# First group's second product wholly dense, and a new order, in a fused linear-attention and feed-forward kernel

## The chip, the cores and the metric

The kernel runs on one core of a Trainium2 chip. The metric is the device time of that core in microseconds, the median of the runs shown. Engines: TensorE (PE, with its weight loads PEld), VectorE (DVE), ScalarE (ACT), GpSimd (POOL) and SyncE (SP), on whose queue nearly all transfers are issued.

## What is computed

Linear attention with a cosine weighting, then two matrix products with a leaky relu between them. Eight batches, eight heads, 576 positions, 64 features per head; 4608 tokens of 512 go through 512 to 2048 to 512.

```python
def phi(x, c, s):
    r = np.maximum(x, 0.0)
    return np.concatenate([r * c, r * s], axis=-1)
q_p, k_p = phi(q, cos_w, sin_w), phi(k, cos_w, sin_w)
kv = np.einsum('bhsf,bhsd->bhfd', k_p, v)
z = np.sum(k_p, axis=2)
num = np.einsum('bhsf,bhfd->bhsd', q_p, kv)
den = np.einsum('bhsf,bhf->bhs', q_p, z)[..., None] + 1e-06
...
h = x @ w_in
g = np.maximum(0.01 * h, h)
return (g @ w_out).astype(np.float32)
```

## The kernel before

The tokens are worked in nine groups of 512: group g below 8 is the first 512 positions of batch g, group 8 the last 64 positions of all eight. Every operation has a short name, and a string `ORDER` lists all names in the order in which they are written into the program, with a letter for the engine where there is a choice (`:D` VectorE, `:A` ScalarE, `:P` GpSimd). Each engine, and the SP queue with its loads and stores, works its own part of that list strictly in order. Nothing else schedules.

The names, by stage:

- Loads: `Lq`, `Lk`, `Lv` bring a batch's q, k, v into one of four staging buffers in rotation (`stage`, 77 to 80 in the order listings), `Lw1.*` and `Lw2.*` the weights w_in and w_out. In groups 0 and 1 k and v come in halves a and b; in group 0 q too. A load into a buffer waits until the earlier content has been read.
- `q{g}.{j}.c` and `.s` (L246, L244) are relu times cosine or sine for token tile j of q, `k...` and `kp...` the same for k, `v...` the cast of v. `K` (L462, L474) sums k and v over the positions on TensorE, `kv` copies the sum out.
- `T{g}.{j}` transposes q on TensorE in groups 0 and 1 (L541), `tc` copies the transposed tile out; later groups do it by a transposing DMA, `Tq`. `N` multiplies q by kv (L562, L573), `D` divides by the denominator (three VectorE instructions, L582 to L586), `X` transposes the result (L598, L613), `xc` copies it out; from group 3 on a DMA, `Tx`, does that.
- First product of group 0: `M{m}` (L665), dense, 16 tiles of 128 rows of w_in; `a0` to `a7` (L674) are the leaky relus into the buffer G.
- First product of groups 1 to 8: `P{g}.{u}.{n}` (L763), seven products instead of eight, for four units u, each of four 256-column matmuls. Between them lie, per unit, the copies `b`, `s`, `u` and the sums `y`, `z` (L234, L238, L240), and the leaky relus `a`, `c`, `e`, `d` (L783). `b` copies the first product into another bank, `u` takes the sum after product 6, `z` and `y` add, and product 4 is added last, after `y`. `Xs`, `Ws` are the sums of inputs that the scheme needs.
- Second product of groups 1 to 8: `F{g}.{n}.{tt}.{h}` (L852), the same scheme over w_out, with sums `S` of G, `Tw` of w_out, copies and sums `t1`, `t2`, `t3`, results `r` and stores `st`.

Second product of group 0, before: w_out and G have 16 tiles to sum over. The first eight are done densely, `E{tt}.0` to `E{tt}.3`, each two matmuls of 512 columns (L688), for four token tiles tt in banks 4 to 7, and `ec{tt}` copies each bank to the result buffer `osb`. The other eight go by the seven products, `F0.n.tt.1`, four matmuls of 256 columns each, 14 operations, in banks 5 and 7; `S0.1h` to `S0.4h` are their sums of G, `t1.0`, `t2.0`, `t3.0` their chain, `r0.*` and `d0.*` add them to what lies in `osb`, and `st0.2` to `st0.5` store four quarters.

PSUM has eight banks of 512 columns: h0 (0, 1), h1 (2, 3), o (4, 5), n (6, 7), as the pools name them. `split.*` and `join.*` change whether two banks are one tile or two. In group 1 the units of the first product use banks by a list of their own, `FIRST_BANKS`, which takes all eight; from group 2 on they rotate through banks 0 to 3. `idle.at.n.id` (L378) are n matmuls of zeros into bank `at`, whose result nobody reads.

Of the kernel before, what the change touches and what calls it, by code (L numbers as in the profile page):

```python
# [20 lines left out]
setup blank:D Lq0b q0b.0.c:P Lk0b q0b.1.s:A Lq0a idle.5.14.0 k0b.1.c:A q0b.1.c:A kp0.3.s:D q0a.1.c:A Lk0a Lv0a  # L21
q0b.3.s:D q0a.1.s:A Lv0b k0b.7.c:D q0b.3.c:A q0a.3.s:D q0a.0.s:A q0b.2.c:P q0b.2.s:D q0a.3.c:A k0b.3.c:A
idle.4.11.1 T0.3 v0.1:A q0b.0.s:A q0a.0.c:D T0.1 k0b.0.c:P k0b.2.c:P T0.0 kp0.0.c:D q0a.2.c:P touch kp0.1.s:D
v0.0:A kp0.0.s:D kp0.1.c:D q0a.2.s:A tc0.1:D k0b.5.c:D k0b.8.c:A k0b.6.c:D tc0.0:D k0b.4.c:A kp0.2.s:D v0.3:P
Lw1.0 idle.5.2.2 K0a cw1.0:P kv0a:A v0.2:P T0.2 N0a.0 tc0.3:A tc0.2:D D0a.0 idle.5.6.3 K0b Lw1.2 Lw1.6 N0a.1
Lw1.1 Lw1.8 Lw1.3 kv0b:A N0b.0 X0a.0 D0a.1 idle.2.2.4 N0b.1 D0b.0 xc0a.0:A X0a.1 idle.2.2.5 X0b.0 M2.0.0
cw1.1:A M0.0.0 M1.0.0 M2.0.1 M0.0.1 xc0a.1:D M3.0.0 M3.0.1 xc0b.0:A D0b.1 cw1.3:D M2.1.0 Lw1.5 M2.1.1 cw1.6:P
Lw1.4 M1.0.1 cw1.2:A M3.1.0 cw1.5:P M0.1.0 M3.1.1 M0.1.1 M1.1.0 M2.0.2 X0b.1 xc0b.1:D M1.1.1 M2.0.3 M0.0.2
M0.0.3 Lq1 M1.0.2 M1.0.3 M0.1.2 cw1.4:D Lw1.7 M3.0.2 M0.1.3 M3.0.3 Ws0.1:D cw1.8:A Ws0.2:D M1.1.2 Ws0.4:D
M1.1.3 a0 M2.1.2 M4.0 Lw2.0 M2.1.3 q1.2.c:D M5.0 Lk1a M3.1.2 M3.1.3 a1 q1.0.s:D M6.0 M7.0 M6.1 M7.1 q1.1.s:D  # L30
M8.0 q1.0.c:D a3 cw1.7:D M8.1 M9.0 Lw2.1 M4.1 Lk1b M9.1 Ws0.3:D q1.3.s:A q1.3.c:A Ws1.1:D M10.0 M5.1 M10.1
M11.0 a4 q1.1.c:D M11.1 Ws1.2:D a2 M12.0 a5 cw2.0.0:D cw2.0.1:A M12.1 q1.2.s:A cw2.1.1:P M13.0 Lv1a M13.1
# [12 lines left out]
P1.2.3 y1.2:D F0.5.0.1 P1.3.2 u1.3:A v2.0:A s1.3:A c1.2 F0.5.1.1 v2.1:P t3.0:D k2.1.s:P d0.5:D k2.2.s:A P1.3.7
Tq2.1 Lk3 F0.4.0.1 S1.1l:D F0.4.1.1 P1.2.4 e1.2 d1.2 r0.5:D k2.0.c:D y1.3:D c1.3 F0.3.0.1 F0.3.1.1 d1.1 P1.3.3
r0.4:D join.n Lv3 r0.3:D P1.3.4 a1.3 z1.3:D S1.2l:D e1.3 S1.1h:D K2 d1.3 F1.1.0.0 kv2:A q3.2.s:A q3.1.s:A
q3.0.s:A F1.6.0.0 F1.1.0.1 S1.3l:D N2.0 F1.1.1.0 S1.2h:D q3.0.c:P F1.1.1.1 Lv3n D2.0 F1.6.0.1 t1.1:A q3.3.s:P
F1.6.1.0 st0.2 N2.1 S1.3h:D q3.3.c:A k3.2.s:P F1.6.1.1 D2.1 F1.2.0.0 t2.1:D F1.2.0.1 st0.3 k3.3.c:A q3.1.c:A
q3.2.c:A Lk3n v3.1:P N2.2 D2.2 Tw4.0:D F1.2.1.0 k3.0.s:A F1.7.0.0 Lq4 F1.2.1.1 F1.7.0.1 N2.3 k3.1.c:A D2.3  # L50
F1.7.1.0 r1.2:A F1.7.1.1 F1.5.0.0 X2.0 k3.2.c:A X2.1 t3.1:D X2.2 X2.3 v3.0:A S1.4l:D F1.5.0.1 xc2.0:D k3.1.s:A
k3.3.s:P F1.4.0.0 xc2.1:A F1.5.1.0 S1.4h:D P2.0.1 F1.4.0.1 Lk4 xc2.2:A k3.0.c:D xc2.3:D F1.5.1.1 b2.0:A
k3.4.c:A P2.0.2 Xs2.1:D Xs2.2:D P2.0.5 P2.0.6 Xs2.3:D k3.4.s:P K3 k4.0.s:P Tq3.0 a2.0 r1.5:D u2.0:A s2.0:D
P2.1.1 kv3:A Xs2.4:D z2.0:D P2.0.7 Tq3.1 k4.0.c:D P2.0.3 k4.1.s:D k4.4.c:A F1.3.0.0 N3.0 Lv4 k4.3.c:P k4.2.s:A
F1.3.0.1 y2.0:D P2.1.5 P2.0.4 e2.0 b2.1:A q4.1.c:A D3.0 P2.1.6 s2.1:A u2.1:A q4.0.s:P N3.1 q4.3.c:D D3.1 Lv4n
P2.1.2 P2.1.3 q4.1.s:P q4.3.s:D P2.1.7 F1.4.1.0 z2.1:D d2.0 F1.3.1.0 a2.1 c2.0 y2.1:D v4.0:P P2.2.5 N3.2
# [920 lines left out]
```

## Time and profile before

| what | value |
|---|---|
| median of 3 runs | 277.11 us (277.1 to 277.85) |
| profiled execution: its own time | 279.91 us |
| span in that profile | 278.1 us |
| TensorE busy | 266.3 us, 96% of the span |
| VectorE, ScalarE, GpSimd busy | 225.9, 192.9, 99.3 us |
| HBM read, written | 36.70 MB, 9.44 MB |
| TensorE's share of the chain that ended last | 76% |

Busy time of TensorE counts matmuls by modelled ends that overlap; a matmul of 256 columns lasts 0.27 us in the profile, but the next starts well before it ends. So the price of one in a row of equal ones is the spacing of the starts: the length of the row, less one duration, through the number less one.

Rows of a timeline give start, length, engine, line, operation, what it writes and reads, shapes and count; in brackets the idle time of that engine before it and what ended the wait. Rows of groups give the count, then busy us and mean ns of one.

### The profile page before, as it was taken

What the parts mean: (1) busy time and instruction counts of PE and PEld (TensorE: products, weight loads), DVE (VectorE), ACT (ScalarE), POOL (GpSimd) and SP (SyncE); (2) the same over time, 40 slices, a digit from 0 to 9 for tenths busy, and PEclk for the clock granted to TensorE, in tenths of its full rate; (3) what the DMA queues carried; (4) which work ended last, traced back from release to release, by engine and by line L of the source; (5) the groups of instructions that cost most, each with busy time, mean ns of one, the idle gap of its engine ahead of it and who ended that gap; (6) DMA issues with size and microseconds to landing.
All of it is one profiled execution on the core that took longest, in us unless ns stands there. A gap on an engine that the chain in (4) does not pass through costs nothing.

```text
span 278.1 us, 7012 instructions
## 1 busy us (share of the span) xinstructions
PE 266.3 (96%) x2813; PEld 232.6 (84%) x2813; DVE 225.9 (81%) x443; ACT 192.9 (69%) x342; POOL 99.3 (36%) x72
## 2 busy tenths in 40 slices
PE   6999999699999999999999999999999999999994
PEld 2566567498889999999999899989999999999983
DVE  1987989789999899989968998879878659866752
ACT  6757998599987887777868788647755555655400
POOL 4631062899375833963544265007100000000000
PEclk9999999799999999999999999999999999999999
DMA  6999999969899999999997996694455206101224
GB/s 231 382 390 383 374 304 347 290 201 247 265 286 170 323 212 230 335 170 261 294 333 127 245 175 217 131 213 116 82 106 154 79 2 151 57 21 40 77 61 131
DMA packets 88145, 57.08 MB, mean 205 GB/s; under 512 B 53808, under 2 KB 83504, under 8 KB 87600
## 3 DMA queue, kind: packets, MB, share of 16 engines
q1 hardware_dynamic: 87504, 56.11, 74.5%
q10 hardware_dynamic: 608, 0.52, 0.7%
q8 instruction: 22, 0.36, 0.5%
q14 instruction: 11, 0.09, 0.1%
HBM read 36.70 MB, written 9.44 MB: 166 GB/s over the span
## 4 chain that ended last, share of the span: by engine, by line
PE 76%; DMA 10%; DVE 7%; ACT 3%; issue 2%; SPq 1%; DVEq 0%; ACTq 0%
PE h L763 29%; PE o L852 29%; PE h L665 4%; DMA stage<-in_q_dram 3%; DMA stage<-in_v_dram 3%; PE n L562 2%; DMA qpT<-qp 2%; DMA xT<-xs 2%; PE n L474 2%; PE n L852 2%; DVE ext L234 1%; PE h L852 1%; ACT g L783 1%; DVE xs L586 1%; DVE h L234 1%
## 5 line engine op out<-in xcount | busy, mean ns | idle before, releaser
L783 ACT ACTIVATE g<-h 128x512 f16<-128x512 f32 x90 | 51.8, 598 | 28.9 <-PE h L763 14.3
L852 PEld LDWEIGHTS <-g 128*128 128x128 f16 x680 | 65.5, 98 | 7.3 <-issue 0.4
L852 PE MATMUL o<-w,g 128*128 128x256 f16 x504 | 68.6, 273 | 0.2 <-DVE osb L234 0.2
L763 PEld LDWEIGHTS <-w 128*128 128x128 f16 x512 | 55.8, 114 | 4.9 <-issue 3.4
L763 PE MATMUL h<-xT,w 128*128 128x256 f16 x356 | 51.0, 274 | 0.0
L763 PEld LDWEIGHTS <-wext 128*128 128x128 f16 x384 | 42.1, 114 | 1.4 <-issue 0.2
L852 PE MATMUL o<-T,ext 128*128 128x256 f16 x232 | 32.9, 273 | 0.4 <-DVE osb L234 0.4
L246 POOL TENSOR_SCALAR qp<-stage,sin_t 128x512 f16<-128x512 f32 x12 | 25.1, 2096 | 15.2 <-DVE xs L586 8.8
L246 POOL TENSOR_SCALAR qp<-stage,cos_t 128x512 f16<-128x512 f32 (+1 forms) x11 | 20.1, 1832 | 28.7 <-DMA stage<-in_q_dram 20.1
L852 PEld LDWEIGHTS <-ext 128*128 128x128 f16 x272 | 26.2, 98 | 3.6 <-issue 0.6
L234 DVE TENSOR_TENSOR h<-h,u 128x512 f32<-128x512 f32 x31 | 21.5, 694 | 9.3 <-PE h L763 5.9
L763 PE MATMUL h<-X,wext 128*128 128x256 f16 x180 | 26.5, 272 | 0.2 <-ACT h L238 0.2
L246 POOL TENSOR_SCALAR kp<-stage,sin_t 128x512 f16<-128x512 f32 (+1 forms) x9 | 18.1, 2018 | 12.0 <-DMA stage<-in_k_dram 6.2
L783 ACT ACTIVATE g<-y 128x512 f16<-128x512 f32 x32 | 20.3, 635 | 2.0 <-DVE y L234 1.8
L238 ACT COPY u<-h 128x512 f32<-128x512 f32 x23 | 13.5, 589 | 11.7 <-PE h L763 11.4
L234 DVE TENSOR_TENSOR y<-h,s 128x512 f32<-128x512 f32 x29 | 19.8, 682 | 2.3 <-PE h L763 1.6
L586 DVE TENSOR_TENSOR xs<-n,rden 128x512 f16<-128x512 f32 x30 | 20.7, 691 | 1.0
L763 PE MATMUL h<-xT,wext 128*128 128x256 f16 x124 | 18.6, 273 | 0.0
L238 ACT COPY h<-h 128x512 f32<-128x512 f32 x25 | 14.5, 580 | 5.0 <-PE h L763 4.6
L852 PE MATMUL o<-ext,g 128*128 128x256 f16 x128 | 17.9, 273 | 0.0
L763 PE MATMUL h<-X,w 128*128 128x256 f16 x116 | 17.4, 272 | 0.1
L246 POOL TENSOR_SCALAR kp<-stage,cos_t 128x128 f16<-128x128 f32 (+2 forms) x12 | 16.9, 1411 | 1.1 <-DMA stage<-in_k_dram 0.8
(144 smaller groups left out, 467.0 us busy)
## 6 DMA issues: line engine op xcount, KB each, us to landing
out_dram<-osb SPq DMA_DIRECT2D x32, 256.0 KB, 3.0
stage<-in_q_dram SPq DMA_DIRECT2D x7, 1024.0 KB, 7.7
stage<-in_k_dram SPq DMA_DIRECT2D x6, 1024.0 KB, 7.1
stage<-in_v_dram SPq DMA_DIRECT2D x6, 1024.0 KB, 8.9
stage<-in_moe_w_out_dram SPq DMA_DIRECT2D x4, 1024.0 KB, 10.9
stage<-in_k_dram SPq DMA_DIRECT2D x4, 576.0 KB, 8.8
stage<-in_v_dram SPq DMA_DIRECT2D x4, 576.0 KB, 6.6
ext<-in_moe_w_in_dram SPq DMA_DIRECT2D x4, 512.0 KB, 9.4
```

The source lines that it names most:

```text
L234: eng.tensor_tensor(out=o, in0=a, in1=b, op=how)
L238: nc.scalar.copy(o, i)
L246: eng.tensor_scalar(out=o, in0=i, scalar1=0.0, scalar2=col, op0=ALU.max, op1=ALU.mult)
L474: nc.tensor.matmul(ps[:, h // NC, (h % NC) * NE : (h % NC + 1) * NE], lhsT=kps[sl, s, :], rhs=vms[sl, s, :], start=start, stop=stop, skip_ ...
L562: nc.tensor.matmul(pairs["n"][lo:hi, h // 4, (h % 4) * NE : (h % 4 + 1) * NE], lhsT=qpT[j // 2][:, j % 2, h, lo:hi], rhs=kv[b][:, h, :],)
L586: nc.vector.tensor_tensor(out=o, in0=ps[:, :, 0 : 4 * NE].rearrange("p a (b e) -> p a b e", e=NE)[:, :, :, 0:D], in1=r.rearrange("p (a b) ...
L665: nc.tensor.matmul(ps[:, m % 2, lo:hi], lhsT=w1[m // 4, c // 2][:, c % 2, m % 4 : 512 : 4], rhs=xT[0][:, lo // P : hi // P, c, :], start=( ...
L763: nc.tensor.matmul(ps[:, mi * HT : (mi + 1) * HT], lhsT=a[:, c, 2 * r0 + mi : 512 : 4], rhs=b[:, c], start=(n in (1, 5) and mi == 0 and c ...
L783: nc.scalar.activation(G[g % 2][:, m : m + 2, r * HT : (r + 1) * HT], {"a": A, "c": y22, "e": E, "d": B_}[e].rearrange("p (m t) -> p m t", ...
L852: nc.tensor.matmul(ps[:, tt], lhsT=a[:, i, tt * P : (tt + 1) * P], rhs=b[:, i], start=(first and i == at and (apart or tt == 0)), stop=(i ...
```

## The change

The second product of group 0 is wholly dense. `E{tt}.0` to `E{tt}.7` sum over all 16 tiles in banks 4 to 7, `ec{tt}` copies out, and `st0.{tt}` stores a token tile of 512 columns at once; there are four such stores as before, with the same bytes. All of group 0's `F0`, `S0`, `t`, `r0` and `d0` operations are gone. Group 1's first product uses banks 0 to 3 like the later groups. Two new one-matmul operations, `clear.1` and `clear.2`, write zeros to banks 1 and 2 ahead of that product. `split.n` and `join.n` are gone. The list `ORDER` is new from end to end; choices of engine change with it. TensorE has 2787 matmuls instead of 2813, and 33 zero matmuls of `idle` instead of 37.

```diff
 def ffn2(tt, lo, hi, eng):
...
                 start=(m == 0),
-                stop=(m == NPR - 1),
+                stop=(m == NFT - 1),
...
+    def store_tile(tt, eng):
+        rows = out[0:MAIN, :].rearrange("(p j) d -> p j d", j=J)
+        nc.sync.dma_start(rows[:, tt], osb[:, tt])
...
-        for i in range(4):
+        for i in range(8):
             op(f"E{tt}.{i}", ffn2, tt, 2 * i, 2 * i + 2)
         op(f"ec{tt}", lambda tt, eng: copy(osb[:, tt], bank[4 + tt], eng), tt)
+        op(f"st0.{tt}", store_tile, tt)
...
-    FIRST_BANKS = ((4, 5, 7), (6, 3, 4), (0, 1, 6), (2, 3, 0))
...
     def banks(g, u):
-        if g == 1:
-            return [bank[i] for i in FIRST_BANKS[u]]
         at = 3 * (4 * g + u)
         return [bank[(at + i) % 4] for i in range(3)]
...
-    for g in range(NG):
+    for g in range(1, NG):
         for n in range(1, 8):
...
-            if g == 0 and t is not None:
-                op(f"d{g}.{n}", tt_op, first_quarter(n), first_quarter(n), half(t), ALU.add)
...
-    op("split.n", change, ("n",), 2)
-    op("join.n", change, ("n",), 1)
+    for at in (1, 2):
+        op(f"clear.{at}", lambda at, eng: idle(at, 1), at)
```

Of the new `ORDER`, one line from the start:

```diff
+k0b.5.c:P idle.5.14.0 k0b.4.c:D T0.2 touch tc0.3:A tc0.1:D v0.0:D T0.0 k0b.2.c:D k0b.6.c:D tc0.0:A Lw1.0
```

What this moves, at three places. First TensorE at the start of the program, before: `osb` are the zero matmuls, `ident,qp` the transposes of q (`T0.3` into n, `T0.1` into h_0_72, `T0.0` into h_0_68), `vm,kp` the sum `K0a`. Weight loads and repeats are left out.

```order
L378 MATMUL o_64<-osb 128x512
...
L378 MATMUL o_63<-osb 128x512
...
L541 MATMUL n_76<-ident,qp_94 128x128
...
L541 MATMUL h_0_72<-ident,qp_93 128x128
...
L541 MATMUL h_0_68<-ident,qp_93 128x128
...
L462 MATMUL h_0_72<-vm,kp 128x66
```

There 14 and 11 zero matmuls stand ahead of the first transpose. The same place of TensorE now (`T0.2` writes o_63):

```order
L377 MATMUL h_0_68<-osb 128x512
...
L540 MATMUL n_76<-ident,qp_94 128x128
...
L540 MATMUL h_0_72<-ident,qp_93 128x128
...
L377 MATMUL o_64<-osb 128x512
...
L540 MATMUL o_63<-ident,qp_94 128x128
...
L540 MATMUL h_0_68<-ident,qp_93 128x128
...
L461 MATMUL h_0_72<-vm,kp 128x66
```

Now 9 zero matmuls stand ahead of `T0.3`, 2 between `T0.3` and `T0.1`, and 14 between `T0.1` and `T0.2`; two more follow `T0.0`.

Second, ScalarE where the first product of group 1 begins, before: `s`, `u` and the copy into o_63 are the copies between products, `g<-` the leaky relus, `qp<-stage_80` the preparation of q of batch 2.

```order
L238 COPY s_119<-o_64 128x512
L244 ACTIVATE qp_93<-stage_80,sin_t 128x8x64
L238 COPY u_118<-n_767 128x512
L244 ACTIVATE qp_94<-stage_80,cos_t 128x8x64
L783 ACTIVATE g_101<-o_63 128x2x256
```

And now, at the same place (`kp<-stage_77` is k of batch 2):

```order
L243 ACTIVATE kp<-stage_77,cos_t 128x8x64
L237 COPY s_119<-h_1_797 128x512
L243 ACTIVATE kp<-stage_77,sin_t 128x8x64
L237 COPY u_118<-h_0_801 128x512
L783 ACTIVATE g_101<-h_0_796 128x2x256
L243 ACTIVATE qp_94<-stage_80,cos_t 128x8x64
L243 ACTIVATE kp<-stage_77,cos_t 128x4x64
L783 ACTIVATE g_101<-h_1_797 128x2x256
```

The first q row of batch 2 stood ahead of the first `u`; now it stands behind `u` and the first leaky relu, and a k row of batch 2 stands ahead of the first `s`. The row `q2.0.s` is on VectorE now, ahead of that unit's `z` and `y`.

Third, SP's loads from the last parts of v of batch 1 on, before:

```order
L325 DMA stage_78<-in_moe_w_out_dram 128x2048
L325 DMA stage_79<-in_moe_w_out_dram 128x2048
L273 DMA stage_80<-in_q_dram 128x8x256
L296 DMA stage_77<-in_k_dram 64x4x64 x2
L289 DMA stage_77<-in_k_dram 128x8x256
```

And now:

```order
L324 DMA stage_78<-in_moe_w_out_dram 128x2048
L324 DMA stage_79<-in_moe_w_out_dram 128x2048
L288 DMA stage_77<-in_k_dram 128x8x256
L272 DMA stage_80<-in_q_dram 128x8x256
L295 DMA stage_77<-in_k_dram 64x4x64 x2
```

The main part of k of batch 2 is now loaded ahead of q of batch 2.

223 lines of the change are left out of this document (105 added, 118 removed).

## The prediction

> **What bounds the kernel now.** First the busy time by stretches, cut at the points on which the sum rests (columns: stretch, length, then busy us and instructions of TensorE, its weight loads, VectorE, ScalarE, GpSimd; granted clock; DMA share; GB/s).
>
> ```profile
> 0.00:19.48 19.48, 16.40 (x185) 8.86 (x186) 12.34 (x33) 12.40 (x25) 9.85 (x20) 1.00 0.92 330
> 19.48:46.41 26.93, 26.69 (x267) 16.79 (x265) 23.36 (x47) 23.28 (x34) 7.22 (x7) 1.00 0.99 358
> 46.41:56.00 9.59, 6.96 (x52) 5.70 (x50) 7.23 (x14) 5.57 (x11) 7.12 (x5) 0.82 1.03 292
> 56.00:71.49 15.49, 15.11 (x167) 14.09 (x164) 14.65 (x25) 14.64 (x27) 13.29 (x8) 1.00 0.84 220
> 105.00:273.90 168.90, 168.09 (x1753) 156.88 (x1750) 136.80 (x264) 107.65 (x195) 42.42 (x23) 1.00 0.62 152
> ```
>
> From 19.48 us, where the first dense matmul starts, to 273.9 us TensorE is the bound: 168.09 of 168.90 us late on, 26.69 of 26.93 early. So the end moves with three things: when that stream starts, how much TensorE work stands in it, and the holes in it. The one large hole is in 46.41 to 56.00. TensorE's own timeline there (start, length, instruction, count, idle time before and its releaser), and what ScalarE and the DMA did:
>
> ```profile
> 49.39 0.60 PE L763 MATMUL o<-xT,w 128*128 128x256 f16 x4 [0.38 <-DVE xT L240]
> 52.24 1.01 PE L763 MATMUL n<-xT,w 128*128 128x256 f16 x4 [2.25 <-ACT u L238]
> 53.05 1.91 PE L763 MATMUL h<-X1b,wext 128*128 128x256 f16 x8
> 54.75 0.95 PE L763 MATMUL h<-xT,w 128*128 128x256 f16 x4
> 55.54 0.60 PE L763 MATMUL n<-xT,w 128*128 128x256 f16 x4
> ```
>
> ```profile
> 47.61 0.59 ACT L238 COPY s<-o 128x512 f32<-128x512 f32 x1
> 51.00 0.72 ACT L244 ACTIVATE qp<-stage,sin_t 128x512 f16<-128x512 f32 x1 [2.79 <-DMA stage<-in_q_dram]
> 51.62 0.57 ACT L238 COPY u<-n 128x512 f32<-128x512 f32 x1
> ```
>
> ```profile
> 41.36 9.55 DMA stage<-in_q_dram
> ```
>
> ScalarE's `q2.0.s` waits for q of batch 2, which lands at 41.36 + 9.55 = 50.91; `u1.0` is queued behind it, and TensorE waits 2.25 us for `u1.0`. Then the clock falls: 16 matmuls take 52.24 to 55.54, 3.30 us, where the next spacing is (0.60 - 0.27) / 3 = 0.109 us and 16 would take 1.74. The hole costs 0.38 + 2.25 + 1.56 = **4.2 us**.
>
> **The change part by part. (1) The second product of group 0.** Two rows give the prices:
>
> ```profile
> 35.95 1.03 PE L688 MATMUL o<-w,g 128*128 128x512 f16 x4
> 272.05 1.91 PE L852 MATMUL h<-w,g 128*128 128x256 f16 x16
> ```
>
> A 512-column matmul follows the last by (1.03 - 0.38) / 3 = 0.217 us, a 256-column one by (1.91 - 0.27) / 15 = 0.109 us. In: 32 dense matmuls, 6.94 us. Out: 14 operations `F0` of 4, 6.10 us. The two `clear` matmuls add 0.43, and four transposes (`X0b.0`), before ahead of the first dense matmul and now behind it, add 0.22. All of it is on the path: **+1.5 us**.
>
> What leaves VectorE and ScalarE with it (four `S0`, three `t`, four `r0`, three `d0`) is 14 operations at rows such as these:
>
> ```profile
> L234 DVE TENSOR_TENSOR osb<-o,osb 128x512 f32<-128x512 f32 x3 | 2.0, 680 | 0.0
> L234 DVE TENSOR_TENSOR osb<-osb,ext 128x512 f32<-128x512 f32 x3 | 2.0, 682 | 0.0
> ```
>
> That is 14 x 0.68 = 9.5 us, but neither engine is the bound: it pays only through the waits that end. One such wait shows:
>
> ```profile
> 65.27 0.60 PE L852 MATMUL o<-T,ext 128*128 128x256 f16 x4 [0.38 <-DVE osb L234]
> ```
>
> `F0.5` waits there for `r0.2` to free its bank: **-0.4 us**. Against that, the first product of group 1 loses its eight banks for four. The stores of group 0 keep their number and bytes, and nothing on TensorE waits for them.
>
> **(2) The start.** The blank matmuls moved. Before, 25 ran while the first loads came in; now 9 do, and 14 stand between two transposes of q, after the data have come:
>
> ```profile
> 2.23 8.24 PE L378 MATMUL o<-osb 128*128 128x512 f16 x25 [2.23 <-DVE osb L413]
> 10.30 0.61 PE L541 MATMUL n<-ident,qp 128*128 128x128 f16 x8
> 12.96 0.74 PE L462 MATMUL h<-vm,kp 64*128 64x66 f16 x36
> 19.48 2.09 PE L665 MATMUL h<-xT,w 128*128 128x256 f16 x16
> ```
>
> The blanks by form, from 2 to 7.3 us and from 7.9 to 10.3 us:
>
> ```profile
> L378 PE MATMUL o<-osb 128*128 128x512 f16 x12 | 5.3, 632 | 2.2 <-DVE osb L413 2.2
> ```
>
> ```profile
> L378 PE MATMUL o<-osb 128*128 128x512 f16 x12 | 2.8, 379 | 0.0
> ```
>
> A blank costs (5.3 - 0.63) / 11 = 0.425 us at half clock and 0.22 at full. ScalarE decides when the transposes can start:
>
> ```profile
> 7.97 0.51 ACT L244 ACTIVATE qp<-stage,cos_t 128x256 f16<-128x256 f32 x1 [0.69 <-DMA stage<-in_q_dram]
> 8.39 0.49 ACT L244 ACTIVATE qp<-stage,sin_t 128x256 f16<-128x256 f32 x1
> ...
> 9.98 0.39 ACT L244 ACTIVATE kp<-stage,cos_t 128x128 f16<-128x128 f32 x1
> ...
> 14.02 1.02 ACT L238 COPY qpT<-n 128x1024 f16<-128x1024 f16 x1
> 16.62 0.38 ACT L238 CAST kv<-h 128x264 f16<-128x264 f32 x1 [1.58 <-PE h L462]
> 17.73 0.59 ACT L238 COPY xT<-o 128x512 f16<-128x512 f16 x1 [0.73 <-PE o L598]
> 20.17 1.05 ACT L238 CAST w<-stage 128x1024 f16<-128x1024 f32 x1
> ```
>
> Half rows of q take 0.40 each on ScalarE. Three run before the second half of q lands (7.95, as now: the same bytes come in the same sizes), five more end at 10.1 (`T0.3` may start), and with a k row (0.39) between, three more end at 11.65 (`T0.1`). The 9 blanks last from 2.23 to 6.1, then TensorE stands idle for 4 us; the 2.25 us hole was enough to halve the clock, so I take half clock from 10.1 on: `T0.3`, two blanks and `T0.1` to 12.7. After the hole half clock lasted until about 55.4, 3.2 us, at the start until about 7.5, 5.3 us: full clock returns between 13.3 and 15.4. I take 14.5, inside that bracket: 4.2 blanks at 0.425, the rest at 0.22, end 16.6 (bounds: 16.0 and 17.1; all at full clock 15.2 from a `T0.1` at full clock, all at half 18.7).
>
> From there: `T0.2`, `T0.0` to 17.5 (8 x (0.61 - 0.22) / 7 = 0.45 each); ScalarE, which has waited for `T0.0`, does `tc0.0` to 18.65, a k row, `tc0.2` to 19.95, a k row, the cast `cw1.2` to 21.3 and `kv0b` to 21.65 (the rows above, 0.95 to 1.0 for the long ones back to back). So `N0b.0` at 21.7, `X0a.0` at 21.95, its copy to 22.95, two blanks, first dense matmul at 23.4 (22.8 to 23.9) instead of 19.48: **+3.9 us** (3.3 to 4.4). Nothing hides it, since the stream behind is TensorE's own; w_in is there by then.
>
> The Trainium skill, TensorE: Matmul & The Clock Gate, Part 1, "What's actually happening", says that the gate judges free-running windows of about 3.4 us. By that rule the return falls between 13.5 and 16.9, differing from execution to execution, and this term would be +3.4 to +5.1; the 3.2 us after the hole agrees, and no run here shows a 4 us gap.
>
> **(3) The hole.** Loads now come as k of batch 2, then q; `q2.0.s` sits on VectorE and `q2.3.c` on ScalarE, behind the work of the first unit. The casts on which the loads wait come 3.9 us later too. GpSimd's rows show how fast they land:
>
> ```profile
> 43.50 1.04 POOL L240 CAST w<-stage 128x1024 f16<-128x1024 f32 x1 [2.62 <-DMA stage<-in_moe_w_out_dram]
> ...
> 47.68 2.22 POOL L240 CAST w<-stage 128x1024 f16<-128x1024 f32 x2 [3.14 <-DMA stage<-in_moe_w_out_dram]
> ```
>
> 4.2 us for a w_out quarter, 50.91 - 47.68 = 3.2 for q. With all of it 3.9 later and k's 3.2 ahead, q lands at 58.0 at the latest; with only w_out's casts late and its queue empty, at about 55. Unit 1 starts in the new stream (dense work by the prices above) at about 52.5, and walking its operations in order, `z1.0`, a weight sum and `y1.0` stand on VectorE behind `q2.0.s`, three steps of 0.6 after its 0.4 (VectorE's `y` by the page's group):
>
> ```profile
> L234 DVE TENSOR_TENSOR y<-h,s 128x512 f32<-128x512 f32 x29 | 19.8, 682 | 2.3 <-PE h L763 1.6
> ```
>
> `y1.0` is what `P1.0.4` waits for, due at 58.85: in time if q lands by 56.5. I take 56.9, between the ends: 0.4 us of wait in place of the 4.2. **-4.2 + 0.4**. Else the stretch has 39 TensorE operations (16.8 us) over 30 of ScalarE (about 16) and 29 of VectorE (about 15.7), where before 44 stood over 39 and 36: tight, but with TensorE still the longest.
>
> **Sum**: +1.5 - 0.4 + 3.9 - 4.2 + 0.4 = **+1.2 us**. Later groups are only reshuffled: 0.8 us of idle time from 105 on bounds a gain, and the same I allow for a loss. The profiled execution took 279.91 (span 278.1), 2.8 over the median; the difference goes on the median: 277.11 + 1.2 = **278.3 us**.
>
> **Rivals.** *Not slower: the blanks are cheap.* If TensorE is back at full clock for them, they end at 15.2, the stream starts at 21.9 (+2.4), and if q is in time, the 0.6 us of idle time from 19.48 to 71.49 outside the hole goes and the 0.8 after 105 too: 2.4 + 1.5 - 4.2 - 0.6 - 0.8 = -1.7, 275.4 us. For it: ScalarE and VectorE lose 9.5 us of work. Against: half clock after a shorter gap. It decides when full clock is back by about 12.7. With half of that, 277 us, no change.
>
> *Clearly slower: the hole comes back.* q lands at 58.0, `P1.0.4` waits 1.5 us instead of 0.4, ScalarE's `e1.0` and `b1.1` behind `q2.3.c` wait as well, and the clock halves for 16 matmuls (1.6): 278.3 + 1.1 + 1.6 = 281.0. For it: same queue, same load. Against: dense matmuls stand ahead of `P1.0.4`. It decides at 56.5 for q.
>
> *The change does not do what it says*: the 14 operations may leave no wait at all, if `F1`'s first bank waits for `ec1` instead; then only the 0.4 is lost, 278.7.
>
> **How the numbers follow.** Forecast 0.50 with the last rival in it (own range 277.4 to 279.6: the start's bounds and 0 to 1 us for q), hole back 0.13, cheap blanks in full 0.15, in part 0.22. About 0.3% (0.8 us) is what a measurement can tell from no change: slower beyond it has most of the forecast and all of the returned hole, 0.49; faster the cheap blanks and some of the part, 0.22; within it 0.29. The range leaves out half of each end: **275.7 to 280.5 us**.
>
> **What would show it.** Right: first dense matmul at 23 to 24 us, blanks of some 630 ns after the second transpose group, TensorE's 2.25 us wait for `u` gone, 64 matmuls on the dense second product. Wrong: dense work starting before 22, a wait of over 1 us on TensorE between 52 and 70 us, or over 2 us more idle time after 105.

## The result, and the profile after

| | before | after |
|---|---|---|
| median, us | 277.48 (277.1 to 277.85, 4 runs) | 282.38 (280.91 to 282.85, 4 runs) |
| profiled execution, us (span) | 279.91 (278.1) | 282.44 (280.5) |
| first dense matmul, us | 19.48 | 23.71 |

After takes 1.0157 of the time before (95% interval 1.0117 to 1.0197): 4.4 us more by this ratio and 4.9 by the medians, where 1.2 were forecast. In a later series it was 1.0206 (1.0164 to 1.0249). Ratios leave out executions over 1.5% above the fastest of the same kernel, medians and ranges do not; where the two say different things, both are given below.

TensorE's timeline of after at the start (start, length, instruction, count, idle time before and its releaser), which answers to the four rows of before from 2.23 to 19.48 us:

```profile
2.22 4.02 PE L377 MATMUL h<-osb 128*128 128x512 f16 x9 [2.22 <-DVE osb L412]
10.44 1.01 PE L540 MATMUL n<-ident,qp 128*128 128x128 f16 x8 [4.20 <-ACT qp L243]
11.25 1.06 PE L377 MATMUL o<-osb 128*128 128x512 f16 x2
12.10 1.06 PE L540 MATMUL h<-ident,qp 128*128 128x128 f16 x8
12.96 3.89 PE L377 MATMUL o<-osb 128*128 128x512 f16 x14
16.68 0.61 PE L540 MATMUL o<-ident,qp 128*128 128x128 f16 x8
...
23.71 1.04 PE L664 MATMUL h<-xT,w 128*128 128x256 f16 x8
```

Nine blanks run, then TensorE waits 4.2 us. The transposes run at half clock (1.01 us for eight, where the row at 16.68 has 0.61), and the 14 blanks follow when ScalarE's rows are already there. These blanks last 16.68 - 12.96 = 3.72 us; at 0.425 and 0.22 each that is three at half clock and eleven at full, so full clock came back at 12.96 + 3 x 0.425 = 14.2. The granted clock of this profile shows 1.00 throughout the first 24 us, also where eight transposes take 1.01 us; here only the lengths of the rows tell the clock.

TensorE's waits behind that, each from the timeline:

```profile
59.50 0.60 PE L763 MATMUL h<-X,w 128*128 128x256 f16 x4 [0.48 <-DVE y L233]
...
105.44 0.63 PE L763 MATMUL h<-xT,w 128*128 128x256 f16 x4 [1.18 <-DMA xT<-xs]
...
158.18 0.63 PE L763 MATMUL h<-xT,w 128*128 128x256 f16 x4 [1.51 <-DMA xT<-xs]
```

The first is `P1.0.4`, the others are `P3.0.1` and `P5.0.1`, the first products on a new group's x. In the profile of before no product waits for that transfer. By stretches (length, busy us and matmuls of TensorE, granted clock):

```profile
52.00:70.00 18.00, 16.88 (x126) 1.00 0.98 255
70.00:105.00 35.00, 34.19 (x444) 1.00 1.08 269
105.00:275.00 170.00, 167.81 (x1752) 1.00 0.66 152
```

TensorE is idle for 1.1 us where group 1's first units run, and for 0.8 and 2.2 us in the two stretches behind. Behind 105 us that is 1.4 more than the 0.8 of before.

### The profile page after: what moved, and what is told of

It is laid out like the page before. It is cut to its first block, busy times and chain, and to the rows that moved or that the text cites. A ratio compares the mean times of both kernels' runs of the same rounds, so it can differ in the third digit from the quotient of the medians.

```text
span 280.5 us, 6942 instructions
## 1 busy us (share of the span) xinstructions
PE 265.3 (95%) x2787; PEld 230.5 (82%) x2787; DVE 223.2 (80%) x440; ACT 185.7 (66%) x327; POOL 103.0 (37%) x76
## 4 chain that ended last, share of the span: by engine, by line
PE 76%; DMA 13%; DVE 6%; issue 2%; ACT 2%; SPq 0%; DVEq 0%; ACTq 0%
PE o L849 30%; PE h L763 29%; DMA stage<-in_q_dram 6%; DMA xT<-xs 4%; PE h L664 4%; PE n L561 2%; DMA qpT<-qp 2%; PE o L377 2%; PE n L473 1%; PE h L849 1%; PE n L849 1%; DVE h L233 1%; PE h L540 1%; ACT qp L243 1%; PE n L687 1%
## 5 line engine op out<-in xcount | busy, mean ns | idle before, releaser
L783 ACT ACTIVATE g<-h 128x512 f16<-128x512 f32 x96 | 55.8, 598 | 39.8 <-PE h L763 22.0
L849 PEld LDWEIGHTS <-g 128*128 128x128 f16 x640 | 61.5, 98 | 6.8 <-issue 0.3
L849 PE MATMUL o<-w,g 128*128 128x256 f16 x480 | 65.5, 273 | 0.0
L763 PE MATMUL h<-xT,w 128*128 128x256 f16 x384 | 54.9, 273 | 2.8 <-DMA xT<-xs 2.7
L245 POOL TENSOR_SCALAR qp<-stage,sin_t 128x512 f16<-128x512 f32 (+1 forms) x12 | 23.1, 1925 | 44.9 <-DMA qpT<-qp 18.8
L245 POOL TENSOR_SCALAR kp<-stage,cos_t 128x512 f16<-128x512 f32 (+2 forms) x15 | 25.2, 1681 | 9.6 <-DMA stage<-in_k_dram 9.6
L233 DVE TENSOR_TENSOR y<-h,s 128x512 f32<-128x512 f32 x32 | 21.9, 684 | 5.4 <-PE h L763 3.1
L237 ACT COPY h<-h 128x512 f32<-128x512 f32 x29 | 16.6, 574 | 5.1 <-PE h L763 4.5
L237 ACT COPY s<-h 128x512 f32<-128x512 f32 x28 | 16.5, 589 | 4.1 <-PE h L763 3.0
L449 POOL TENSOR_SCALAR vm<-stage 128x1152 f16<-128x1152 f32 (+1 forms) x15 | 14.8, 1000 | 8.0 <-DMA stage<-in_v_dram 8.0
```

What stands on the lines that cost most here:

```text
L233: eng.tensor_tensor(out=o, in0=a, in1=b, op=how)
L237: nc.scalar.copy(o, i)
L245: eng.tensor_scalar(out=o, in0=i, scalar1=0.0, scalar2=col, op0=ALU.max, op1=ALU.mult)
L449: POOL.tensor_scalar(out=o, in0=i, scalar1=1.0, scalar2=0.0, op0=ALU.mult, op1=ALU.add)
L763: nc.tensor.matmul(ps[:, mi * HT : (mi + 1) * HT], lhsT=a[:, c, 2 * r0 + mi : 512 : 4], rhs=b[:, c], start=(n in (1, 5) and mi == 0 and c ...
L783: nc.scalar.activation(G[g % 2][:, m : m + 2, r * HT : (r + 1) * HT], {"a": A, "c": y22, "e": E, "d": B_}[e].rearrange("p (m t) -> p m t", ...
```

## The experiments

Names are those of `ORDER`. An edit is shown by the names that move; a line of "..." stands for what lies between.

**Before, once more.** No edit: a second profile of the same kernel.

> The kernel before, unchanged, for a second profile. Theory 'the hole is common': again some 4 us are lost on TensorE where group 1's first product begins (a wait of over 2 us for u1.0 and half clock behind it), and the execution takes about what its unprofiled runs take. Rival 'the hole was this one execution's': q of batch 2 lands earlier, the wait is under 1 us, the clock stays, and the span is 2 to 3 us shorter than the 278.1 us of the first profile.

It took 276.98 us (span 275.2). TensorE's busy time by stretches of this profile, and its wait for `u1.0`:

```profile
46.00:66.00 20.00, 17.79 (x160) 1.00 1.03 271
66.00:100.00 34.00, 33.57 (x439) 1.00 1.02 263
100.00:270.00 170.00, 169.18 (x1766) 1.00 0.63 153
```

```profile
49.60 0.60 PE L763 MATMUL o<-xT,w 128*128 128x256 f16 x4 [0.38 <-DVE xT L240]
51.18 0.60 PE L763 MATMUL n<-xT,w 128*128 128x256 f16 x4 [0.98 <-ACT u L238]
```

The hole is 0.38 + 0.98 = 1.4 us here, with a granted clock of 1.00 over the whole stretch, where the first profile had 4.2 with half clock. TensorE's idle time is 2.2 us in the units' stretch and 0.4 and 0.8 behind, against 1.1, 0.8 and 2.2 of after: the new order waits less there and more later. The difference between the two holes is 2.8 us. That first profiled execution (279.91) stood by the same 2.8 over its median (277.11), and its span is 2.9 longer than this one's. Of the two expectations the rival came, with the wait only just under the 1 us that it gave.

**The hole filled in the kernel before.**

```diff
-q2.0.s:A P1.0.2 Lk2 u1.0:A P1.0.7 q2.3.c:A Tw1.1:D q2.2.s:P a1.0 Lv2n q2.1.c:D q2.1.s:P
+P1.0.2 Lk2 u1.0:A P1.0.7 Tw1.1:D q2.2.s:P a1.0 Lv2n q2.1.s:P
...
-y1.0:D Tw3.0:D
+y1.0:D q2.1.c:D Tw3.0:D
...
-s1.1:A P1.1.6
+s1.1:A q2.0.s:A q2.3.c:A P1.1.6
```

> The kernel before, with the preparations q2.0.s and q2.3.c on ScalarE moved behind that engine's first copies and relus of group 1, and q2.1.c on VectorE behind y1.0: the wait for q no longer stands ahead of u1.0. Theory 'the hole is common and costs 4 us': 273 to 274 us. Rival 'the hole was the profiled execution's alone': 276 to 277.5 us, under 1.5 us of gain.

276.98 us against 277.39 (12 runs), ratio 0.9987 (0.9967 to 1.0006). TensorE's wait for `u1.0` is gone, and a 0.68 us wait for another operand stands 5 us later:

```profile
50.03 0.60 PE L756 MATMUL n<-xT,w 128*128 128x256 f16 x4
...
55.24 0.60 PE L756 MATMUL n<-X,w 128*128 128x256 f16 x4 [0.68 <-DVE X L227]
```

In the median, filling the hole is worth 0.4 us, 0.9 at the interval's end, and not 4.2.

**The blanks ahead of the transposes again.** After, with one name moved.

```diff
-idle.0.9.1 T0.3 q0b.1.s:A kp0.3.s:D idle.5.2.2 T0.1 k0b.5.c:P idle.5.14.0 k0b.4.c:D
+idle.0.9.1 idle.5.14.0 T0.3 q0b.1.s:A kp0.3.s:D idle.5.2.2 T0.1 k0b.5.c:P k0b.4.c:D
```

> The changed kernel with the 14 zero matmuls back ahead of the first transpose. Theory 'the start lies on the path': the first dense matmul comes at about 19.2 us instead of 23.7, and the whole is 4.0 to 4.5 us faster than the changed kernel, about 278 us. Rival 'the late start hid the loads': q or k of batch 2 is now late for group 1's first product, 1 to 3 us of new waits stand there between 47 and 66 us, and the gain is 1 to 3 us.

TensorE's timeline of that kernel:

```profile
5.96 3.19 PE L370 MATMUL o<-osb 128*128 128x512 f16 x14
10.83 0.61 PE L533 MATMUL n<-ident,qp 128*128 128x128 f16 x8 [1.69 <-ACT qp L236]
...
19.14 1.03 PE L657 MATMUL h<-xT,w 128*128 128x256 f16 x8
```

277.82 us against 277.39 (12 runs), ratio 0.9986 (0.9962 to 1.001). Most of the blanks lie in the wait and at full clock, the transposes too, and the dense work starts at 19.14 instead of 23.71. A little of the rival holds as well, earlier than it was looked for: in seven of the ten profiles with the blanks moved, and in none with the late start, TensorE waits 0.3 to 1.1 us at 38 to 40 us for GpSimd's cast of v of batch 1. The longest of these waits, from one of the kernels further down:

```profile
39.11 0.75 PE L454 MATMUL h<-vm,kp 64*128 64x66 f16 x36 [1.10 <-POOL vm L442]
```

The same kernel was run twice more, as the measure for others:

> The kernel after with the 14 blanks ahead of the transposes, once more, as the measure for the two kernels run beside it. It took 277.8 us in an earlier series against 277.4 of before. If the late start is all that made the change slower, it is again within 0.5% of before; if that series was a lucky one, it comes to 279 or more, and the rest of the change costs some 1.5 us as well.

> The kernel after with the 14 blanks ahead of the transposes, a third time, as the measure for the two beside it: two series gave medians of 277.8 and 279.6, with 8 of 24 executions over 280. The same is expected here, 278 to 279.5, with some 4 of 12 over 280.

Ratios 1.0045 (1.0015 to 1.0074) and 1.0027 (0.9994 to 1.006). Over the three series this kernel stands by the ratios 0.5 us over before, between 0.4 under and 1.2 over. By the medians (277.82, 279.56 and 278.99) it stands 0.4, 2.0 and 1.3 over, and the second of them is past the 279 at which the expectation called the first series a lucky one. After itself took 282.91 beside that second series. So the place of one name carries 3.4 to 4.7 us of the 4.4 to 5.7, and what the rest of the change brings lies between nothing and 2 us.

**That part of the change alone.** Before, with the same 14 blanks moved back.

```diff
-Lq0a idle.5.14.0 k0b.1.c:A
+Lq0a k0b.1.c:A
...
-T0.1 k0b.0.c:P
+T0.1 idle.5.14.0 k0b.0.c:P
```

> The kernel before with that part of the change alone which moves the 14 blank matmuls from ahead of the transposes to behind the second group of transposes. If the late blanks are the loss by themselves, TensorE stands idle for some 3 us ahead of the transposes, runs the transposes and most of the blanks at half clock, the first dense matmul comes at 22.5 to 24 instead of 19.5, and the time is 3 to 4.5 us over before (280.4 to 282). If the loss needs the order of q and k rows of the kernel after (all four transposes late), the first dense matmul comes before 21.5 and the time is under 279.4.

```profile
10.07 0.62 PE L533 MATMUL n<-ident,qp 128*128 128x128 f16 x8 [2.97 <-ACT qp L236]
10.53 0.93 PE L533 MATMUL h<-ident,qp 128*128 128x128 f16 x8
11.25 4.58 PE L370 MATMUL o<-osb 128*128 128x512 f16 x14
...
23.16 2.09 PE L657 MATMUL h<-xT,w 128*128 128x256 f16 x16
```

281.42 us against 277.8, ratio 1.0135 (1.0105 to 1.0164): 3.7 us, and the first dense matmul comes 23.16 - 19.48 = 3.7 us later. The late blanks are the loss by themselves, in either order.

**After without the 14 blanks.**

```diff
-T0.1 k0b.5.c:P idle.5.14.0 k0b.4.c:D T0.2
+T0.1 k0b.5.c:P k0b.4.c:D T0.2
```

> The kernel after without the 14 blank matmuls (zero times zero; nothing of the output hangs on them). If they cost only because they stand on TensorE's path, the first dense matmul comes at 19.5 to 20.5 and the time is 277.5 to 278.5, as with the blanks moved ahead. If they are worth their time for the clock, TensorE is at half clock through the transposes and the projection until 18 us or later and into the dense matmuls, and the time is 279.5 to 281.

279.16 us against 277.58, ratio 1.0067 (1.0041 to 1.0093). The dense work starts at 20.13 us; the transposes run at half clock to 14 us and the dense work does not. So the start came as the first theory has it, and the time 0.7 us over what it gave. For `P2.0.7` now waits, which it hardly does in after (0.24 us at most), and `P3.0.1` waits longer:

```profile
85.30 0.60 PE L763 MATMUL h<-xT,w 128*128 128x256 f16 x4 [1.48 <-ACT u L237]
103.76 0.63 PE L763 MATMUL h<-xT,w 128*128 128x256 f16 x4 [1.49 <-DMA xT<-xs]
```

The start came 3.6 us earlier, and the time is 3.2 us less by the medians, 2.5 by the first ratio of after and 3.9 by the later one.

**More and less dense work.** Both on the kernel with the blanks moved: eight of the 64 dense matmuls left out, or eight matmuls of zeros added.

```diff
-        for i in range(8):
+        for i in range(7):
             op(f"E{tt}.{i}", ffn2, tt, 2 * i, 2 * i + 2)
...
-                stop=(m == NFT - 1),
+                stop=(m == NFT - 3),
```

```diff
+    zeros = sb("zeros", [P, 448], F16)
...
+    def ffn2_more(tt, eng):
+        for _ in range(2):
+            nc.tensor.matmul(
+                bank[4 + tt][:, 0:448], lhsT=zeros[:, 0:P], rhs=zeros, start=False, stop=False
+            )
+        ffn2(tt, 14, 16, eng)
...
-        for i in range(8):
+        for i in range(7):
...
+        op(f"E{tt}.7", ffn2_more, tt)
```

> The kernel after with the 14 blanks ahead of the transposes, and with a part of the work left out: the second product of group 0 sums 14 of its 16 row blocks, so 8 of 64 dense matmuls are gone, 8 x 0.217 = 1.74 us of TensorE. If TensorE's work lies wholly on the path, as the +1.5 us of the sum supposes, it takes 276.1 us against 277.8. If in this stretch ScalarE and VectorE set the pace and the dense matmuls only fill TensorE's waits, the waits at P1.0.4, P1.1.3 and P1.2.6 grow instead and the time falls by less than 0.6.

280.26 us against 277.8 (6 runs), ratio 1.011 (1.0062 to 1.0158): more, with less work, as neither theory has it. Since its base had been run in another series, it was run again beside it, with the opposite edit:

> The same with 8 of the 64 dense matmuls of group 0's second product left out (14 of 16 row blocks summed), 1.74 us less of TensorE. Its first series, beside other kernels, gave 280.3, more than the 277.8 with all of them. If TensorE's work lies on the path, it is now 1.7 us under the kernel run beside it; if the dense matmuls only fill waits for ScalarE and VectorE, it is within 0.6 of it; over it by 1 us or more only if the shift of later work against the loads costs time of its own.

> The same with 8 matmuls of zeros (448 columns, 8 x 0.217 x 448 / 512 = 1.52 us) added to the dense second product, two at the end of each of its four sums; the output is not changed by them. If TensorE's work lies on the path, 1.5 us over the kernel with the blanks moved alone; if it fills waits, the waits at P1.1.3, P1.2.6 and P1.0.4 shrink and the time rises by less than 0.6.

Side by side: base 1.0045 (1.0015 to 1.0074), less 1.0044 (1.001 to 1.0077), more 1.003 (1.0002 to 1.0058); the medians are 279.56, 278.87 and 278.25. The 3.3 us of TensorE work between the two ends do not appear in the time: the kernel with the most work comes out lowest by both, within the noise. TensorE from 52 to 66 us, for base, less and more (stretch, length, busy us and matmuls, granted clock):

```profile
52.00:66.00 14.00, 12.91 (x96) 1.00 0.92 230
```

```profile
52.00:66.00 14.00, 11.68 (x84) 1.00 0.87 229
```

```profile
52.00:66.00 14.00, 12.99 (x94) 1.00 0.90 230
```

With less work the idle time grows from 1.09 to 2.32 us. Two waits of the kernel with less show it; base has 0.24 and 0.28 at the same operations, `P1.1.3` and `P1.2.6`, and the kernel with more has none there:

```profile
58.37 0.60 PE L756 MATMUL h<-xT,wext 128*128 128x256 f16 x4 [0.67 <-DVE s L232]
61.84 0.60 PE L756 MATMUL h<-X,wext 128*128 128x256 f16 x4 [0.71 <-ACT h L230]
```

0.43 more at each, which is the price of the two matmuls left out ahead of each. In this stretch VectorE and ScalarE set the pace, and dense matmuls fill waits. Behind it `P2.0.7` waits again for ScalarE, 1.34 us in the kernel with less and 0.28 in base, so the rest of the work left out is waited for there.

**The products that wait for x moved back.** After, with `P3.0.1`, `P3.1.1`, `P3.0.5` and `P5.0.1`, `b5.0` behind products that need no new x.

```diff
-P3.0.1 Xs3.1:D F2.1.0.1 Xs3.2:D Tq4.1 F2.1.1.0 e2.3 F2.1.1.1 S2.1h:D b3.0:A P3.0.2 kv4:A P3.1.1 t1.2:A P3.0.6 P3.0.5
+Xs3.1:D F2.1.0.1 Xs3.2:D Tq4.1 F2.1.1.0 e2.3 F2.1.1.1 P3.0.1 P3.1.1 S2.1h:D b3.0:A P3.0.5 P3.0.2 kv4:A t1.2:A P3.0.6
...
-P5.0.1 kv6:A q7.1.c:A P4.3.4 c4.3 e4.3 Lk7 b5.0:A F3.4.1.1 k7.0.s:P N6.0 F3.3.0.0 Xs5.2:D F3.3.0.1
+kv6:A q7.1.c:A P4.3.4 c4.3 e4.3 Lk7 F3.4.1.1 k7.0.s:P N6.0 F3.3.0.0 Xs5.2:D F3.3.0.1 P5.0.1 b5.0:A
```

> The changed kernel with the first products of groups 3 and 5 (P3.0.1, P5.0.1) put behind three or four second-product operations that need nothing of the transposing DMA. Theory 'the two waits for xT cost the end 3 us': TensorE's 2.7 us wait for xT goes and the whole is 2.3 to 3.0 us faster than the changed kernel, about 279.7 us. Rival 'they only move': the products that follow wait for the copies b3.0 and b5.0 or for their sums instead, gain under 1 us.

> The kernel after with the products on transposed x moved back, once more, for a second profile: its median was 282.75, its profiled execution 278.96. If the clock's return sets the spread, an execution at 282 to 283 shows the first dense matmul at 23.5 or later (22.4 in the first profile) and waits behind it as before (1.3 us after 105). If the waits set it, the first dense matmul stands at 22.4 again and 3 us of waits come back behind 105 us.

> The kernel after with both edits: the 14 blank matmuls right behind the first nine, and the products P3.0.1 and P5.0.1 (with their companions) behind the products that need no new x. If the two waits for transposed x (1.3 and 0.2 us in the profile with the blanks moved) are a loss of their own, this comes to 276.4 us, 1.4 under the 277.8 of the blanks alone and 1 under before. If removing a wait only brings the next one, as the moves without the blanks suggest (no gain in the median), it stays within 0.5 of 277.8.

On after: 282.75 us (7 runs), ratio 1.0195 (1.0165 to 1.0225), no gain; one execution took 278.96, a second profile 282.08. With the blanks moved as well: 279.8, ratio 1.0075 (1.0048 to 1.0103), slower than the blanks alone. That kernel's waits behind 70 us:

```profile
119.54 0.60 PE L842 MATMUL o<-ext,g 128*128 128x256 f16 x4 [0.65 <-DVE ext L226]
144.39 0.60 PE L842 MATMUL o<-T,ext 128*128 128x256 f16 x4 [1.34 <-DVE osb L232]
156.51 1.05 PE L842 MATMUL o<-w,g 128*128 128x256 f16 x8 [0.67 <-DVE g L226]
158.71 0.60 PE L756 MATMUL h<-X,wext 128*128 128x256 f16 x4 [0.28 <-ACT h L230]
```

No wait for x, and 2.9 us of waits for VectorE and ScalarE, whose sums now stand closer to their users. Of the two profiles on after, the one of 278.96 has 0.9 us of waits behind 70 us and its first dense matmul at 22.41, the one of 282.08 has 2.3 and 23.61. So neither expectation on the second profile held in full: the later start and longer waits, 1.55 us for VectorE's sum at 158, came together.

**After, profiled and timed again.**

> The kernel after once more, for a second profile. If its time over before is the late start and TensorE's added work, the first dense matmul stands again at 23 to 24 us with half clock until at least 13.5, and the time is 281 to 283. If the return of full clock differs from execution to execution by a window of 3.4 us, the first dense matmul may stand at 22.4 instead, and the time 1.3 us lower.

> The kernel after itself, timed beside the others: 281 to 283 us, 1.3 to 1.9% over before, if the late start costs what it did; 280 or less only if the series before had many executions with a late return of full clock.

The second profile took 279.86, with the first dense matmul at 23.2, 1.17 us of wait for x at `P3.0.1` and none at `P5.0.1`: the start is as the first theory has it, the time 1.1 us under its range. The series took 282.91 (281.2 to 285.01), ratio as given above; its profile has the first dense matmul at 22.90. Over the five profiles with the late start in this order it lies between 22.41 and 23.71.

**The transposing load of x of batch 5.** In two of the three profiles of the kernel with the blanks moved, `P5.0.1` waits, 1.67 and 1.80 us; in the third it does not. The timeline of the first, the same operations in the third, and the granted clock of the first:

```profile
154.86 1.04 PE L756 MATMUL h<-xT,w 128*128 128x256 f16 x4 [1.67 <-DMA xT<-xs]
155.70 1.06 PE L756 MATMUL h<-X,w 128*128 128x256 f16 x4
156.55 1.06 PE L842 MATMUL o<-ext,g 128*128 128x256 f16 x4
...
158.96 0.60 PE L756 MATMUL h<-X1b,wext 128*128 128x256 f16 x4
```

```profile
152.97 0.63 PE L756 MATMUL h<-xT,w 128*128 128x256 f16 x4
...
155.43 0.60 PE L756 MATMUL h<-X1b,wext 128*128 128x256 f16 x4
```

```profile
154.80:158.30 3.50, 3.44 (x23) 0.52 0.83 244
158.30:162.00 3.70, 3.70 (x35) 1.00 1.30 222
```

That execution took 280.41 us, the one without the wait 277.5, 2.9 less. The wait of 1.67 and 1.64 of half clock (158.96 - 154.86 = 4.10 us against 155.43 - 152.97 = 2.46 for the same operations) are 3.3, which covers it. The queue of SP in the same profile, and in the kernel that puts `Tx5` ahead of `Tq6.0`:

```profile
143.38 5.21 SPq L539 DMA_TRANSPOSE qpT<-qp  x1
148.68 3.83 SPq L545 DMA_TRANSPOSE xT<-xs  x1
```

```profile
147.65 2.11 SPq L545 DMA_TRANSPOSE xT<-xs  x1
149.93 2.26 SPq L539 DMA_TRANSPOSE qpT<-qp  x1
```

```diff
-D5.3 Tq6.0 e4.2 v6.0:P P4.2.4 F3.7.1.1 b4.3:A P4.3.2 Tx5
+D5.3 Tx5 Tq6.0 e4.2 v6.0:P P4.2.4 F3.7.1.1 b4.3:A P4.3.2
```

> The kernel after with the 14 blanks ahead of the transposes and one more edit: Tx5 ahead of Tq6.0. If the two groups of its times (276 to 278.5 and 280 to 281.4) come from the wait of P5.0.1 for that load, 1.67 us in one profile and 0.2 in another, and the half clock after it, then the upper group goes or gets rarer and the median is 277 or less. If the groups have another cause, the median stays at 278 to 279.5 and half of the times lie over 279.5.

279.38 us (278.69 to 279.73, 6 runs), ratio 1.0054 (1.0033 to 1.0076). The upper group of times went, as expected of the one theory; so did the lower, as expected of neither. The load of x is in time, and `N6.0` waits for the one that it overtook:

```profile
155.40 0.43 PE L554 MATMUL n<-kv,qpT 128*128 128x66 f16 x8 [1.07 <-DMA qpT<-qp]
...
157.82 0.60 PE L756 MATMUL h<-X,wext 128*128 128x256 f16 x4 [0.68 <-ACT h L230]
```

**Several waits mended at once.** First on VectorE and ScalarE alone:

```diff
-q2.0.s:D z1.0:D Tw4.0:D y1.0:D P1.0.4 k2.0.s:P e1.0 k2.2.s:D q2.1.c:D q2.2.c:D b1.1:A s1.1:D
+z1.0:D Tw4.0:D y1.0:D s1.1:D q2.0.s:D P1.0.4 k2.0.s:P e1.0 b1.1:A k2.2.s:D q2.1.c:D q2.2.c:D
...
-ec0:A a1.1 P1.1.7 q2.0.c:D E3.7 e1.1 b1.2:A
+ec0:A b1.2:A a1.1 P1.1.7 q2.0.c:D E3.7 e1.1
...
-z2.2:D F1.3.1.0 N3.3 F1.4.1.1 v4.0:P d2.1 P2.3.1 k4.1.c:D k4.3.c:D P2.2.7 P2.3.5 k4.0.c:A D3.3
+z2.2:D N3.3 D3.3 F1.3.1.0 F1.4.1.1 v4.0:P d2.1 P2.3.1 k4.1.c:D k4.3.c:D P2.2.7 P2.3.5 k4.0.c:A
```

> The kernel after with the 14 blanks ahead of the transposes and the order of VectorE and ScalarE mended at four waits that its trace shows: the half row of q of batch 2 behind y1.0 and s1.1, b1.1 and b1.2 one or two places earlier, and N3.3, D3.3 (the last part of the new x of batch 3) ahead of two k rows. If each wait that the trace shows is time of its own, 0.4 of the 0.48 at P1.0.4, the 0.24 at P1.1.3, the 0.28 at P1.2.6 and at least 0.75 of the 1.26 at P3.0.1 go, and it takes 276.1 us, 1.7 under the blanks alone and 1.3 under before. If a wait that goes only uncovers the next one, as with the products moved behind x, it stays between 277.3 and 279.

278.38 us against 277.8, ratio 1.0013 (0.9988 to 1.0039), as expected if a wait that goes uncovers the next. In this kernel `b1.2` writes the bank that `e1.1` reads after it, so a quarter of the hidden values of unit 1 is another unit's; instructions and sizes are the same. The waits at `P1.0.4`, `P1.1.3`, `P1.2.6` and `P3.0.1` are gone, and these have come:

```profile
60.86 0.60 PE L756 MATMUL h<-X1b,wext 128*128 128x256 f16 x4 [0.92 <-ACT g L776]
98.17 0.60 PE L756 MATMUL h<-X,w 128*128 128x256 f16 x4 [1.46 <-DVE y L226]
154.75 0.63 PE L756 MATMUL h<-xT,w 128*128 128x256 f16 x4 [1.74 <-ACT g L776]
```

Then with `Tx5` ahead and the two k rows behind `y2.2`; of the three moves above only the first is kept, so `b1.2`, `N3.3` and `D3.3` stand as in after:

```diff
-k4.1.c:D k4.3.c:D P2.2.7 P2.3.5 k4.0.c:A D3.3 e2.2 b2.3:A y2.2:D
+P2.2.7 P2.3.5 k4.0.c:A D3.3 e2.2 b2.3:A y2.2:D k4.1.c:D k4.3.c:D
...
-D5.3 Tq6.0 e4.2 v6.0:P P4.2.4 F3.7.1.1 b4.3:A P4.3.2 Tx5
+D5.3 Tx5 Tq6.0 e4.2 v6.0:P P4.2.4 F3.7.1.1 b4.3:A P4.3.2
```

> The kernel after with the 14 blanks ahead of the transposes, the transposing load Tx5 ahead of Tq6.0 in the queue of SP, two k rows of batch 4 behind y2.2 on VectorE (so that D3.3, the last part of x of batch 3, and its load Tx3 come 1.2 us earlier), and the half row of q of batch 2 behind y1.0 and s1.1, with b1.1 one place earlier. If these waits are time of their own, P5.0.1 and P3.0.1 lose some 1 us of wait each and P1.0.4 and P1.1.3 some 0.6 together, and no execution shows half clock near 155 us: 276.5 or less in the median, under before. If they only hand the time on, 278 to 279.5 as the kernel run beside it.

279.29 us against 277.7, ratio 1.0052 (1.0025 to 1.0078), the same as with `Tx5` alone. The waits for x at `P3.0.1` and `P5.0.1` are gone; waits of 1.06 us for q at `N6.0`, 0.80 for VectorE at 99.7 and 0.68 for ScalarE at 157.6 stand there now. No version was faster than before beyond its interval; before with its hole filled (0.9987) and after with the blanks moved, in its best series (0.9986), come nearest.

## Why the prediction was right in direction and wrong in size

**The start: right in size, not shown in its reason.** Forecast +3.9 with the first dense matmul at 23.4 (22.8 to 23.9); it came at 23.71 in the profile, and at 22.41 to 23.61 in four others. The edit alone costs 3.7 us on before and gives 3.4 to 4.7 back on after. Full clock came back at 14.2 where 14.5 was taken. That the gap had halved the clock, as the forecast has it, this profile does not show: the nine blanks ahead of the gap already take 4.02 us, half clock, and no row between them and 14.2 is at full. It is shown in before with the late blanks, whose transposes at 10.07 run at full clock and where the granted clock falls to 0.50 at 10.64.

The rule cited from the Trainium skill gave 13.5 to 16.9, and the 14.2 agrees with it. The four other profiles have 12.9, 13.4, 14.3 and 15.0. The first two lie under that range: there the granted clock fell at 9.46 and 10.02, where the forecast began to count at 10.1. The cheap-blanks rival needed full clock by 12.7. The execution with 12.9 came close to it: its first dense matmul is at 22.41, where the rival had 21.9.

**The hole: the step that failed.** The sum took -4.2 for it, from the one profiled execution, whose 279.91 stood 2.8 over its median, and then put the difference on the median of 277.11. But the half clock and the longer wait, 4.2 - 1.4 = 2.8, were that execution's surplus. The one profiled near the median has 1.4, and filling the hole gains 0.4 in the median. So at least 2.8 of the 4.2 was a gain on a time that the median did not have; the forecast with 1.4 in its place would have been 281.1.

The spans say the same. From the first profile of before to that of after they grow by 2.4 us: 4.2 at the start, and 1.8 less behind it, where +3.9 and -2.7 were forecast. From the second profile of before (275.2, first dense matmul at 19.47) they grow by 5.3: again 4.2 at the start, and 1.1 more behind it.

**Later groups "only reshuffled", 0.8 either way: failed in one profile of three.** Behind 98 us TensorE's waits come to 1.0 and 0.7 us in the two profiles of before, and to 2.9, 1.2 and 1.4 in the three of after. `P3.0.1` waits 1.1 to 1.6 us for the transposing load in every profile that keeps the order around it, and `P5.0.1` from nothing to 2.2, with half clock behind it at times. The order of the queue was at hand: `Tx5` stands behind `Tq6.0` now, whose issue takes 5.2 us of SP, and before it stood ahead. These waits are not simply to be had back, though: with every edit that took one away (products later, load earlier, sums earlier) other waits came, for VectorE, ScalarE or the other load, in most profiles of the same size, and the median was no lower.

**TensorE's added work, +1.5: not found in the time.** The counts stand, but in the stretch of group 1's first units TensorE waits for the other two engines, so 1.7 us less or 1.5 us more of dense work there did not show. The prediction had said that all of it was on the path. This error ran the other way than that of the hole and hid a part of it.

**The wait for q, +0.4: right.** `P1.0.4` waits 0.48 us for `y1.0` in the profile, 0.37 and nothing in two others. VectorE takes up `q2.0.s` at 57.16 us after 1.06 us of waiting for the load, where the forecast had q at 56.9; the rival of the returned hole needed 58.

**The -0.4 at `F0.5`**: that wait is gone, and waits of 0.24 and 0.28 us (`P1.1.3`, `P1.2.6`) stand in its stretch.

Put together from the runs: 3.4 to 4.7 us for the start, and for all else +0.5 by the ratios, 0.4 to 2.0 by the medians, instead of -2.7. Of this the hole's size is shown by the second profile and the filled hole. How much of the rest the waits for x cost in the median stays open: none of the edits that removed them made the kernel faster, but each brought other waits. The signs by which the forecast was to be known as right came (dense work from 23.7, the first late blanks at half clock, no 2.25 us wait for `u`), and none of the signs for wrong: they looked at the trace of after, and most of the error lay in the time of before.

## What to carry to other kernels

Before a stall of one profile is booked as a gain on a median, compare that execution's time with the median: what the stall has over its usual size is already in the difference. Filler work is free only while its engine waits for something else; the same 14 matmuls cost nothing ahead of the data and 3.7 us behind them. And for each load whose issue moves, look at which long issue now stands ahead of it in its queue and how much work is left between issue and first use.

## What the runs showed of the hardware

Half clock came in stretches of one length. In seven profiles the granted clock falls once, to 0.50, and each time it stays there for 3.41 us: in the row from 154.80 to 158.30 shown above, 0.52 granted over 3.50 us is (1 - 0.52) / 0.5 x 3.50 = 3.4, with full clock on both sides. The fall comes within a wait of TensorE (at 9.46 us in a wait from 6.2 to 10.0), at its end (154.90, wait until 154.86) or behind it (157.16, 1.1 us after a wait of 2.21). The length of the wait does not decide alone: at `P5.0.1`, waits of 1.67, 1.80 and 2.21 us were followed by a fall, and waits of 1.51 and 1.74 in two other kernels were not. The Trainium skill, TensorE: Matmul & The Clock Gate, Part 1, "What's actually happening", has free-running windows of that length, and lets the clock fall after an idle one. The length agrees; but half such a window of waiting was enough here, and how short a gap may be that still counts as idle is not seen from these runs.

In the two profiles shown, the issue of a transposing load on SP took 5.21 us for q and 3.83 for x behind it, and 2.11 for x and 2.26 for q in the other order.
